# Router logits of two steps at once on column quarters, and three list products behind the transposes

## The chip, the cores and the metric

One core of one Trainium2 chip. The metric is device time in microseconds (us), the median of several executions. The engines are named as in the profile: PE is the matrix engine, PEld its weight loads, DVE the vector engine, ACT the scalar engine, POOL GpSimd, and SP the engine whose queue issues most of the transfers.

## What is computed

A retention layer (linear attention with a decay per head) over 4 batches of 768 tokens with 8 heads of 64, then a mixture of experts with a router in two levels. Cut to what matters:

```python
for t in range(S):                                   # B=4, H=8, S=768, D=64
    state = gamma * state + einsum('bhd,bhe->bhde', k[:, :, t], v[:, :, t])
    y[:, :, t] = scale * einsum('bhd,bhde->bhe', q[:, :, t], state)
x = y.transpose(0, 2, 1, 3).reshape(3072, 512)
g_logits = x @ w_group                               # 4 groups
g_idx = argmax(g_logits)
for g in range(4):
    e_logits = x[g_idx == g] @ w_expert[g]           # 4 experts in a group
    e_idx = argmax(e_logits)
    for e in range(4):                               # one expert for each token
        out[tok] = g_w * e_w * (relu(x[tok] @ w1[g, e]) @ w2[g, e])
```

The change is in the part that makes the 20 router logits of a token (4 of the groups, 16 of the experts).

## The kernel before, in words

The program has two stages. The first, `attention` (about 100 us), walks 12 steps; a step i holds two blocks of 128 tokens. The second runs the 16 experts with weights that stream from memory. A few instructions of the second (splitting the weights of the first expert) are laid between those of the first. The order on every engine is the order in which the code issues; no scheduler moves anything. So the line of a call in the loop of `attention` sets where it stands in each engine's queue.

A step i of `attention` issues on PE, in this order:

- `score_mm` of step i+1, first block (L240, PSUM banks sh0 and sh1), then `state_out` of step i (L291, queries by the state before), then `score_mm` of step i+1, second block (banks sh2 and sh3). DVE masks the scores out of the four banks into `pf` (`score_mask`, L252, four instructions a step); `pf` has three buffers, so the mask of the second block waits for the first half of step i's value product;
- `value_out` (L304, masked scores by values), then `state_mm` (L266, the new state), and ACT copies the state (L276). Steps 5 and 11 end a sequence, make no new state and need no keys; step 6 starts one and has no `state_out`. `state_mm` reads the keys from `kk`; for steps 9 and 10 (`KEYED`) these come by a transfer (L217), issued when the `state_mm` ahead of it is done; for the others PE transposes them (`keys_mm`, L225);
- `logits_mm` of step i-1 (L324): four products, one for each quarter of the 512 features, each with a stationary `wr` of 128x32 (20 columns used) and a moving `xt` of 128x256. Product j writes the 32 PSUM partitions 32j to 32j+31, so the four stand in four column quarters of the PE array, and each holds a part of the sum. ACT copies the 128x256 result to `ls` (L329). DVE makes `xt` in `out_x` (L316, two instructions a step);
- `keys_mm` of step i+1, then `trans_mm` of step i-1 (L350): `xt` transposed to token order, which ACT copies and SP writes to memory (`xd`);
- `select_mm` of step i-1 (L337): two products, stationary `ls` (128x128), moving a 0/1 matrix of 128x20, which add the four parts and turn the logits to one token a partition, in PSUM bank `log`. In steps 4, 8, 9 and 10 they are put off (`select_late`) into the step behind, among `score_mm`, `state_out` and `state_mm`.

Routing works on batches of two steps (`route`, a generator of small DVE instructions that `route_steps` advances). In an odd step, behind the masks, DVE makes the marks `oh` (L391 to L408) out of bank `log`; then `out_x`; behind the transposes PE counts ranks (L444, L446) into `log`, DVE reads them (L452 to L461), and in the even step weights follow (L421 to L434). `spread` (L527, L515 on DVE, L534 on POOL) and `tally` (L555, four bfloat16 products into `log`, and L562 on DVE, which adds them to `lists`) enter a batch into the experts' lists: `spread` at the end of steps 4, 6 and 8 and at the start of step 10, `tally` in steps 5, 7, 9 ahead of `state_out`, and in step 10.

All matrices of this stage but those of ranks and lists are float32. The trace shows a float32 product as two records, with a load each.

## Time and profile before

| what | us |
|---|---|
| median of 3 runs (394.51 to 395.0) | 394.56 |
| the profiled execution, its own time | 392.61 |
| its span, first to last instruction | 390.9 |

The span starts with the first instruction on any engine. The page lists busy time by engine, the chain of work that ended last (followed back from the end, at each step to what released it), and groups of instructions. The timeline lists instructions in order of time. Each view counts from the start of the span. The profiled execution is 1.95 us below the median of the runs.

### The profile page before, as it was taken

Reading aid. Unit: us, or ns where it says so; the run is one execution under the profiler, and the core shown is the slowest. Engines: PE = TensorE matmul, PEld = TensorE weight load, DVE = VectorE, ACT = ScalarE, POOL = GpSimd, SP = SyncE. Lnnn points to the kernel's source line nnn. Section 1 sums busy time; section 2 is a strip of 40 time slices with the busy share of each in tenths; the row PEclk is TensorE's granted clock in tenths of the full one; section 3 lists DMA queues with packets and bytes.
Section 4 is the critical chain, followed back from the end, with each engine's and each line's share of the span. In section 5 each row is a group of like instructions: output and inputs, shape, how many; then the busy total and the mean of one; then the engine's idle time right before and its main releaser. Section 6 shows DMA issues by size and latency. Waiting matters only on the chain.

```text
span 390.9 us, 14282 instructions
## 1 busy us (share of the span) xinstructions
PE 381.9 (98%) x5945; PEld 322.9 (83%) x5977; DVE 288.5 (74%) x480; ACT 224.3 (57%) x342; POOL 160.2 (41%) x172
## 2 busy tenths in 40 slices
PE   8999999999999999999999999999999999999993
PEld 4888989888869888888888879797887978879792
DVE  3675876868879979795868686776878769788630
ACT  2234534544654766666657667676766767667620
POOL 5533669578766325131425324241531403322112
PEclk9999999999999999999999999999999999999997
DMA  7999999989647998787879797988879798797011
GB/s 254 342 369 325 315 381 321 341 292 305 221 177 259 338 359 269 249 278 257 268 249 274 268 331 251 300 294 305 293 262 352 273 314 300 268 349 263 6 49 50
DMA packets 38042, 107.24 MB, mean 274 GB/s; under 512 B 11415, under 2 KB 11543, under 8 KB 30548
## 3 DMA queue, kind: packets, MB, share of 16 engines
q1 hardware_dynamic: 28752, 92.52, 68.5%
q0 software_dynamic: 8928, 12.63, 9.2%
q8 instruction: 54, 0.88, 0.9%
q10 hardware_dynamic: 292, 1.08, 0.8%
q14 instruction: 16, 0.13, 0.1%
HBM read 94.18 MB, written 13.20 MB: 275 GB/s over the span
## 4 chain that ended last, share of the span: by engine, by line
PE 83%; issue 9%; POOL 3%; DMA 3%; DVE 0%; POOLq 0%; ACT 0%; SPq 0%; DVEq 0%; ACTq 0%
PE hps L918 19%; PE yps L1011 16%; PE hps L898 9%; PE yps L1016 6%; PE op L304 5%; PE sh L240 4%; PE yps L1004 3%; PE tpx L839 3%; PE sh L350 3%; PE stp L266 3%; PE op L291 2%; POOL out L1098 2%; DMA kk<-kt 2%; PE sh L324 1%; PE yps L955 1%
## 5 line engine op out<-in xcount | busy, mean ns | idle before, releaser
L786 DVE TENSOR_TENSOR wl<-wf,wh 128x1024 bf16<-128x1024 f32 x120 | 145.3, 1222 | 38.5 <-ACT wh L784 38.2
L784 ACT ACTIVATE wh<-wf 128x1024 f16<-128x1024 f32 (+1 forms) x136 | 133.6, 1002 | 1.0 <-DMA wf<-w2p 1.0
L918 PE MATMUL hps<-xbh,wh 128*128 128x0 bf16 x544 | 93.3, 241 | 0.0
L918 PE MATMUL hps<-xbh,wl 128*128 128x0 bf16 x544 | 93.3, 241 | 0.0
L1098 POOL DMA_INDIRECT out<-yo,mt x18 | 22.2, 1235 | 102.9 <-ACT yo L1078 100.1
L918 PEld LDWEIGHTS <-wh 128*128 128x128 f16 x616 | 56.5, 98 | 0.1
L925 ACT ACTIVATE hh<-hps 128x256 bf16<-128x256 f32 (+16 forms) x68 | 34.2, 503 | 35.6 <-PE hps L918 35.3
L918 PEld LDWEIGHTS <-wl 128*128 128x128 bf16 x544 | 53.2, 98 | 0.2
L898 PE MATMUL hps<-xbl,wh 128*128 128x256 f16 (+14 forms) x472 | 50.2, 249 | 0.0
L1016 PEld LDWEIGHTS <-wh 128*128 128x128 f16 x448 | 28.6, 97 | 24.9
L252 DVE TENSOR_TENSOR pf<-sh,tri 128x512 f32<-128x512 f32 x48 | 30.6, 685 | 21.8 <-PE sh L240 7.8
L1011 PE MATMUL yps<-wh,hl 128*128 128x512 f16 x112 | 42.5, 380 | 0.0
L1011 PE MATMUL yps<-wl,hh 128*128 128x512 bf16 x112 | 42.4, 379 | 0.0
L1011 PE MATMUL yps<-wh,hh 128*128 128x512 f16 x112 | 42.4, 378 | 0.0
L821 POOL DMA_INDIRECT xg<-xd,mt x22 | 36.8, 1674 | 11.0 <-PE hps L898 2.7
L841 ACT ACTIVATE xbh<-tpx 128x512 bf16<-128x512 f32 (+14 forms) x32 | 16.7, 523 | 42.7 <-PE tpx L839 42.6
L898 PEld LDWEIGHTS <-wh 128*128 128x128 f16 x472 | 40.2, 98 | 0.5
L1016 PEld LDWEIGHTS <-wl 128*128 128x128 bf16 x448 | 28.6, 97 | 13.3
L928 DVE SCALAR_TENSOR_TENSOR hl<-hps,hh 128x216 f16<-128x216 f32 (+15 forms) x64 | 36.8, 576 | 2.7 <-ACT hh L925 2.6
L1098 POOL DMA_INDIRECT out<-yo,gx x8 | 9.5, 1194 | 55.6 <-ACT yo L1078 41.4
L1016 PE MATMUL yps<-hh,wh 128*128 128x0 bf16 x448 | 31.8, 192 | 0.0
L1016 PE MATMUL yps<-hh,wl 128*128 128x0 bf16 x448 | 31.7, 192 | 0.0
(210 smaller groups left out, 632.6 us busy)
## 6 DMA issues: line engine op xcount, KB each, us to landing
wf<-w2p SPq DMA_DIRECT2D x29, 1024.0 KB, 6.3
wf<-w1p SPq DMA_DIRECT2D x28, 1024.0 KB, 6.9
lq<-qkv SPq DMA_DIRECT2D x24, 256.0 KB, 5.8
lk<-qkv SPq DMA_DIRECT2D x24, 256.0 KB, 5.3
lv<-qkv SPq DMA_DIRECT2D x24, 256.0 KB, 5.8
xd<-xr SPq DMA_DIRECT2D x22, 256.0 KB, 4.9
wf<-w1p SPq DMA_DIRECT2D x16, 256.0 KB, 5.9
wf<-w2p SPq DMA_DIRECT2D x8, 256.0 KB, 5.9
```

The source lines that it names most:

```text
L252: nc.vector.tensor_tensor(o, sc, tri, ALU.mult)
L304: nc.tensor.matmul(s["o"][par][64 * half:64 * half + 64, u, pp], s["vs"][:, u, hs], s["pf", u][:, par, p, :], start=(c == 0 and u == 0 and ...
L784: nc.scalar.activation(u["wh"][i][:, cs], u["wf"][i][:, cs], AF.Copy)
L786: (eng or nc.vector).tensor_tensor(u["wl"][i][:, cs], u["wf"][i][:, cs], u["wh"][i][:, cs], ALU.subtract)
L821: nc.gpsimd.indirect_dma_start(out=xg[0:r, i, :], out_offset=None, in_=self.xd[0:n, :], in_offset=bass.IndirectOffsetOnAxis(ap=mt[0:r, i, ...
L898: nc.tensor.matmul(hv[:, a, 0:w], l, xl[:, k, 0:w], start=(k == 0 and a == 0), stop=False, skip_group_check=True)
L918: nc.tensor.matmul(o, l[:, k, fs], m, start=(n == 0 and not arms), stop=(n == len(terms) - 1), skip_group_check=True,)
L925: nc.scalar.activation(hh[:, f, 0:W], hv[:, :, 0:W], AF.Relu)
L928: nc.vector.scalar_tensor_tensor(*rest)
L1011: nc.tensor.matmul(big, h[:, k, 0:P], w[k], start=(n == 0), stop=(n == 23))
L1016: nc.tensor.matmul(o, w[k][:, d * P:d * P + P], m, start=(n == 0 and d == 0), stop=(n == 23), skip_group_check=True,)
L1098: s = nc.gpsimd.indirect_dma_start(out=self.out, out_offset=bass.IndirectOffsetOnAxis(ap=mt[0:r, i, 0:1].bitcast(U32), axis=0), in_=yo[0:r ...
```

## The change

- `logits_mm` and `select_mm` go, and with them the 0/1 matrix of the constants and `select_late`.
- `pair_logits(i)` makes the logits of steps i and i+1 together: 16 products, each with a stationary `wr` of 128x32 and one token block of `xt` as 128 moving columns. Column quarter j holds block j of the four, and the four feature quarters g are added up in PSUM. It is issued in even steps for the two steps before, behind the scores and ahead of `value_out`, into bank sh0; for steps 10 and 11 behind the loop.
- `pair_select` takes the place of four `select_mm` products: two, stationary `ls` (half the tokens of a block, 128x64), moving 80 columns of the identity matrix. It stands behind `state_copy` of the even step.
- `tally` of steps 5, 7 and 9 moves from ahead of `state_out` to behind `trans_mm`.

```diff
-                if i % 2 and not last:
-                    self.select_late()
-                if i in (5, 7, 9):
-                    self.tally()
                 if i > 2:
                     self.state_out(i, 0)
-                if last:
-                    self.select_late()
                 if i > 1:
                     self.state_out(i, 1)
-                if i < NS2 - 2:
-                    self.select_late()
                 if i % 2 == 0:
                     self.route_steps(99, True)
                 if i > 1:
                     scores(i + 1, 1)
+                if i % 2 == 0:
+                    self.pair_logits(i - 2)
...
             self.state_copy(i)
-            if i == 10:
-                self.select_late()
+            if i and i % 2 == 0:
+                self.pair_select()
             beside(i, 4)
-            if i:
-                self.logits_mm(i - 1, 1 if last or i % NC == NC - 2 or i + 1 in KEYED else 2)
             self.out_x(i)
...
             if i:
-                late = i + 1 in KEYED or i % NC == NC - 2
-                self.trans_mm(i - 1, late=late)
...
+                self.trans_mm(i - 1)
+                del self.st[i - 1]
+            if i in (5, 7, 9):
+                self.tally()
...
-            self.logits_mm(last)
+            self.pair_logits(last - 1)
             self.xtrans(ua, "big", (0,))
-            self.select_mm(last)
-            self.trans_mm(last, self.yp, late=True)
+            self.pair_select()
+            self.trans_mm(last, self.yp)
```

The new functions:

```diff
+    def pair_logits(self, i):
+        nc = self.nc
+        if i == NS2 - 2:
+            lt = self.pp.tile([P, 512], F32, name="lgt", tag="sta", bufs=1)[:, 0:P]
+        else:
+            lt = self.sh[0][:, 0:P]
+        for g in range(4):
+            for j in range(4):
+                nc.tensor.matmul(
+                    lt[32 * j:32 * j + 32, :], self.wr[:, g, :], self.xts[i + j // 2][:, g, j % 2],
+                    start=(g == 0), stop=(g == 3), skip_group_check=True,
+                )
+        self.ls = self.wp.tile([P, P], F32, name="ls", bufs=1)
+        nc.scalar.activation(self.ls, lt, AF.Copy)
+
+    def pair_select(self):
+        pick = self.ident.rearrange("p (j c) -> p j c", j=4)[:, :, 0:20]
+        for a in (0, 64):
+            lg = self.log[a:a + 64, LG:LG + 80].rearrange("p (j c) -> p j c", j=4)
+            self.nc.tensor.matmul(lg, self.ls[:, a:a + 64], pick, start=True, stop=True, skip_group_check=True)
```

Three places in the engines' queues (in the changed file the same code stands some lines earlier: L240, L266, L304, L555, L562 are L239, L265, L303, L548, L555 there).

PE in an even step, from the last score product to the key transposes; before (step 6):

```order
L240 MATMUL sh_118<-lq,lk 64x64
L240 MATMUL sh_119<-lq,lk 64x64
L304 MATMUL op<-pf,vs 64x128 x16
L266 MATMUL stp<-vs,kk 64x64 x16
L324 MATMUL sh_118<-xt,wr 32x256 x4
L225 MATMUL sh_116<-ident,lk 128x128 x4
```

and with the change:

```order
L239 MATMUL sh_118<-lq,lk 64x64
L239 MATMUL sh_119<-lq,lk 64x64
L326 MATMUL sh_116<-xt,wr 32x128 x16
L303 MATMUL op<-pf,vs 64x128 x16
L265 MATMUL stp<-vs,kk 64x64 x16
L338 MATMUL log<-ident,ls 64x80 x2
L224 MATMUL sh_116<-ident,lk 128x128 x4
```

The four products of 256 columns behind the state are now 16 of 128 columns ahead of the value product, in bank sh0 (`sh_116`), and two select products stand where the four stood. In an odd step neither stands any more.

DVE in step 7, where the list sum stands; before:

```order
L252 TENSOR_TENSOR pf<-sh_116,tri 128x512
L252 TENSOR_TENSOR pf<-sh_117,tri 128x512
L562 TENSOR_TENSOR lists<-lists,log 128x160
L252 TENSOR_TENSOR pf<-sh_118,tri 128x512
L252 TENSOR_TENSOR pf<-sh_119,tri 128x512
```

and with the change:

```order
L401 TENSOR_TENSOR oh<-log,go 128x64
L315 TENSOR_TENSOR xt<-op,gx 128x512 x2
L555 TENSOR_TENSOR lists<-lists,log 128x160
L445 TENSOR_TENSOR log<-log,nb 128x64
L448 TENSOR_TENSOR nb<-log,nb 128x16
```

The sum stood between the masks of the two score blocks; now it stands behind `oh` and `xt` and directly ahead of the reading of the ranks.

PE at the end of step 10; before:

```order
L350 MATMUL sh_118<-ident,xt 128x128 x4
L350 MATMUL sh_119<-ident,xt 128x128 x4
L291 MATMUL op<-lq,V 64x128 x8
L337 MATMUL log<-rest,ls 128x20 x2
L291 MATMUL op<-lq,V 64x128 x8
L304 MATMUL op<-pf,vs 64x128 x16
```

and with the change:

```order
L345 MATMUL sh_118<-ident,xt 128x128 x4
L345 MATMUL sh_119<-ident,xt 128x128 x4
L290 MATMUL op<-lq,V 64x128 x16
L303 MATMUL op<-pf,vs 64x128 x16
L845 TENSOR_LOAD ecols
```

The select products that split the state products of step 11 are gone.

## Rows read from the trace of the kernel before

**Rows 1.** Page, busy time by engine: us (share of the span) and instructions.

```profile
PE 381.9 (98%) x5945; PEld 322.9 (83%) x5977; DVE 288.5 (74%) x480; ACT 224.3 (57%) x342; POOL 160.2 (41%) x172
```

**Rows 2.** Chain that ended last, in order of time, step 7: start, us, what.

```profile
65.96 1.91 PE op L304 x32
67.87 0.93 PE stp L266 x32
68.81 0.57 PE sh L324 x8
69.37 1.02 PE sh L225 x8
70.40 0.87 PE sh L350 x8
71.27 0.36 PE log L337 x4
71.63 0.04 PE log L444
...
71.76 0.81 PE sh L240 x24
72.57 0.89 PE op L291 x32
73.46 0.65 PE sh L240 x24
```

**Rows 3.** The same chain, step 5's list products; the select products put off to step 11.

```profile
48.54 0.28 PE log L555 x4
48.82 1.03 PE op L291 x32
...
94.63 0.79 PE op L291 x16
95.42 0.55 PE log L337 x4
95.98 0.60 PE op L291 x16
```

**Rows 4.** Timeline, step 4's logits products on PE and their loads: start, us, engine, line, what.

```profile
45.49 0.16 PEld L324 LDWEIGHTS sh<-xt,wr 128*32 128x32 f32 x8
45.49 0.64 PE L324 MATMUL sh<-xt,wr 128*32 128x256 f32 x8
```

**Rows 5.** Line L324, its loads: duration of one, ns, least, median and most.

```profile
L324 PEld LDWEIGHTS sh<-xt,wr x88: 106/108/110, 19.4 to 98.4; 128*32 128x32 f32 x88
```

**Rows 6.** Timeline, steps 9 and 10: start, us, engine, line, what.

```profile
80.65 0.31 DVE L562 TENSOR_TENSOR lists<-lists,log 128x160 f32<-128x160 f32 x1
...
81.85 1.97 PE L304 MATMUL op<-pf,vs 128*64 128x128 f32 x32
...
83.06 1.29 DVE L252 TENSOR_TENSOR pf<-sh,tri 128x512 f32<-128x512 f32 x2 [2.10 <-PE op L304]
...
86.33 1.28 DVE L316 TENSOR_TENSOR xt<-op,gx 128x512 f32<-128x512 f32 x2
...
87.52 0.22 DVE L452 TENSOR_TENSOR log<-log,nb 128x64 f32<-128x64 f32 x1
...
89.73 0.79 DVE L527 TENSOR_TENSOR yT<-rest,tile 128x128 bf16<-128x128 f32 x1
...
91.05 2.47 DVE L252 TENSOR_TENSOR pf<-sh,tri 128x512 f32<-128x512 f32 x4
```

**Rows 7.** The chain again, step 5: value product and rank product.

```profile
50.51 1.06 PE op L304 x16
...
55.78 0.04 PE log L444
```

**Rows 8.** The chain again, the transfer of the keys of step 9.

```profile
77.59 6.23 DMA kk<-kt
...
83.87 1.33 PE stp L266 x32
```

## The prediction, on record before the changed kernel ran

> **What bounds the kernel now.** I read the page first: PE is busy 98% of the span [rows 1], so in general a microsecond less on PE is a microsecond less in all. Then the chain of work that ended last, over the first 100 us. It runs through PE nearly without a break, so in this stage the chain's rows are prices: each is the time by which a group of products moves the end. Step 7 shows a whole step [rows 2]: value product 1.91, state 0.93, logits 0.57, key transposes 1.02, `xt` transposes 0.87, select 0.36, ranks 0.13 (from 71.63 to 71.76), then scores 0.81, state products 0.89, scores 0.65. The step's last row ends where the next value product starts. The third view is the timeline of DVE in the odd steps [rows 6]: there DVE does masks, marks, `xt` and the reading of the ranks one behind the other, and a PE that gets shorter meets a DVE that doesn't.

> A second price stands in the same rows. Transposes behind other transposes take 0.87; of the same count and shape behind the column quarters of the logits they take 1.02 [rows 2]. Scores behind transposes take 0.81, behind state products 0.65. So a change between whole array, halves and quarters costs about 0.15.

> **PE work removed.** Twelve logits groups at 0.57 [rows 2]: 6.84. Twelve select groups: six behind transposes at 0.36 [rows 2], the six others near the 0.55 of the one in step 11 [rows 3]: 5.4. That one also cuts the state products in two: 0.79 and 0.60 [rows 3] in place of 0.89 [rows 2], so 0.5 goes with it. The list products of steps 5, 7 and 9 stand between scores and state products, and behind them the state products take 1.03 [rows 3] against 0.89 [rows 2]; behind transposes no change of shape is left: 3 x 0.14, 0.4. Sum 13.1.

> **PE work added.** `pair_logits`, six times 16 float32 products with 128 moving columns, in four column quarters. The nearest rows are the state products: 16 products, 128 columns, four parts of the array at once, 0.89 [rows 2]. Halving the length of L324 gives the upper end: 16 products of 128 columns are as many columns as two groups of four with 256, 2 x 0.57 = 1.14 [rows 2]. The lower end is 0.85, the 0.89 without its own edges. I take 0.89 and 0.15 for a change of shape, 1.04: the row has the same count of products and of parts. Six of them: 6.24. `pair_select`: two products of 80 columns in two halves, behind the state products, which have the same halves and take 0.93 for 16 of 64 columns [rows 2], 0.058 each. 2 x 0.058 x 80/64 = 0.15, between 0.1 and the 0.36 of today's select. Five of them 0.75; the sixth stands between transposes behind the loop and pays two changes of shape, 0.45. Added in all 7.4, so PE sheds 13.1 - 7.4 = **5.7 us**.

> [...]

> **Waits that it adds.** *Rank products.* They write bank `log`, and so do the list products; the list sum on DVE reads it. In the built program the list products now wait for `oh`, and the first rank product waits for the list sum. That sum stands behind `xt` on DVE. Step 9 gives DVE's times from the start of the value product at 81.85 [rows 6]: second mask at 1.2 (it needs the `pf` buffer that the first half of the value product frees), `xt` from 4.5 to 5.75, so the list sum (0.31 [rows 6]) ends at 6.06, and the ranks start there. Steps 5 and 7 have the same DVE work. PE would be there sooner:
> - step 7: 1.91 + 0.93 + 1.02 + 0.87 + 0.28 for the list products [rows 2, 3] = 5.01. Wait 1.05; before, the ranks came at 5.67 with none [rows 2].
> - step 5 makes no state: 4.08, wait 1.98. Before, its ranks came at 55.78 - 50.51 = 5.27 [rows 7], of which 1.91 + 0.57 + 1.02 + 0.87 + 0.36 = 4.73 is work, so 0.54 is not new: 1.44.
> - step 9 has no key transposes: 1.91 + 0.93 + 1.02 + 0.28 = 4.14, wait 1.92, of which about 0.35 was there (ranks 4.78 behind the value product, work 4.43): 1.57. The transfer of its keys hides in this. It is issued when the state of step 8 is done and takes 6.23 [rows 8]; PE gets to the next state some 0.9 us before it lands, and waits there in place of waiting at the ranks.

> Together 4.06. Queued behind the waiting rank product on PE are the scores, the state products and the pair's logits, and through them the next value product.

> *Logits in step 10.* `pair_logits` writes sh0, so it waits for the first mask of scores that were made just before. In step 10 DVE first finishes the route and the `spread` of steps 6 and 7: from reading the ranks at 87.52 to the masks at 91.05 it takes 3.53 [rows 6], and 0.65 more for the first mask. With 0.13 for the ranks themselves, `pair_logits` can start 4.31 behind their start. PE is there after 0.13 + 0.81 + 0.89 + 0.65 = 2.48 [rows 2]. Wait 1.83, all new: today the value product stands there and needs only masks of the step before. In steps 2, 4 and 8 the mask is ready (DVE has no `spread` in front of it); in step 6, without state products, it is 0.15 late.

> *Behind.* In step 11 the ranks lose the 0.57 of logits that stands ahead of them, and their marks come no sooner; I take 0.5, between 0 and 0.57. For the logits behind the loop, which wait for the last `xt`, 0.1.

> Sum of the waits: 4.06 + 1.83 + 0.15 + 0.6 = **6.6 us**. Costed at nothing: the smaller copy on ACT (ACT has slack, 57% [rows 1]); the later first pair of logits, since `route` starts at the end of the even step as before; the loads of q, k and v, which move with the steps. The experts' stage is bound by PE and shifts as a whole.

> **Sum.** -5.7 + 6.6 = +0.9. The profiled execution would go from 392.6 to 393.5. That execution lies 1.95 below the median of the runs; on the median the forecast is 394.56 + 0.9 = **395.5 us**. What a measurement can tell from no change is 0.2%, 0.8 us, here.

> **Rivals.**
> - *The waits just eat the work.* The same mechanism with DVE a little quicker: the `yT` in step 10 took 0.79 [rows 6] beside POOL, and in another alignment it may be shorter; the wait at step 11 may be 0. Then +0.9 - 0.5 - 0.5 = -0.1, 394.5, no measurable change. For it: my sum is a small difference of two large ones. Chance 0.32.
> - *Faster: DVE's work ahead of the first mask in step 10 is short enough.* It decides at 2.5 us from ranks to finished mask: below that the 1.83 is gone, and the kernel is at 395.5 - 1.8 = 393.7. Against it stand the rows: 3.53 for that stretch, and DVE's order there is unchanged. For it: part of the stretch waits for POOL. Chance 0.17.
> - *PE alone bounds.* The list products find their marks ready and the ranks find the sum ready: -5.7 and the small waits, about 389.4. The order on DVE, where the sum stands behind `xt`, speaks against it. Chance 0.04.
> - *The loads are laid bare in `pair_logits`*, as if rounds on the same rows could not overlap: 0.86 more in each of six groups [rows 5], 395.5 + 5.2 = 400.7. Rows 4 speak against it. Chance 0.04. [...]

> That the change doesn't do what it says I leave out: the order shows the products gone and the new ones in place.

> **How the numbers follow.** Forecast 0.43, the others as given. Slower by over 0.2%: 0.43 + 0.04 = 0.47; within: 0.32; faster: 0.17 + 0.04 = 0.21. The slower case alone runs from 395.4 to 397.3: upper end with 1.14 for the logits (+0.6), 0.36 for the select (+1.0) and waits as computed. The range of 8 in 10 goes on down through no change to the faster case, 393.0, and leaves out the two rivals with 0.04 and a tail: **393.0 to 397.3**.

> **What would show it.** Right: L326 groups of about 1.0 on the chain, selects of 0.15 to 0.2; in steps 5, 7 and 9 the rank products (L437) start 6.0 to 6.2 behind the value product, just behind the list sum; in step 10 PE idle of 1.5 to 2.2 ahead of L326 with a DVE mask as what ended it; the even-to-odd halves of a pair shorter by about 1.4 and the odd-to-even longer. Wrong: no idle time at these places, or an L326 group of 1.5 or more, or a last attention step that ends more than 1.5 us from where it ends now while the list above holds.

## The result, and the profile after

The changed kernel takes 399.03 us (median of 10 runs, 396.43 to 401.45) against 394.63 for the kernel before in the same session (10 runs, 393.07 to 395.81): ratio 1.0108, 95% interval 1.0075 to 1.0142. It is slower by 4.4 us. The forecast was 395.5 with a range up to 397.3: the sign is right, the size is not. The profiled execution took 398.88, close to the median.

The page, busy time by engine, against [rows 1]:

```profile
span 397.1 us, 14370 instructions
...
PE 377.4 (95%) x5974; PEld 322.3 (81%) x6049; DVE 288.6 (73%) x480; ACT 221.5 (56%) x336; POOL 159.3 (40%) x172
```

PE did get shorter by 4.5 us, 381.9 to 377.4. But the span grew, so PE is idle for 10.7 us more than before (397.1 - 377.4 = 19.7, against 390.9 - 381.9 = 9.0). The question is what it is idle for. The chain that ended last, steps 2, 3 and 6 and 7 (start, us, what), against [rows 2]:

```profile
26.13 0.65 issue
26.78 0.66 PE sh L239 x15
27.44 1.01 PE sh L326 x32
28.45 1.90 PE op L303 x32
30.35 0.93 PE stp L265 x32
31.28 0.14 PE log L338 x4
31.42 1.02 PE sh L224 x8
32.44 0.11 PE sh L345
32.55 1.35 issue
33.90 0.98 PE sh L345 x7
...
60.04 1.08 PE sh L326 x32
61.12 1.90 PE op L303 x32
63.02 0.93 PE stp L265 x32
63.95 0.14 PE log L338 x4
64.09 1.03 PE sh L224 x8
```

The prices of the two new groups came out: L326 1.01 to 1.08 (forecast 1.04), L338 0.14 (forecast 0.15). Beside them stand rows named "issue", which [rows 2] don't have: PE stands still in the middle of a group of like products, and no engine and no transfer of data ended it. The waits of PE by line, from 8 us to the end of the attention stage (us in total, times, longest):

```profile
PE log L437 <- DVE lists L555: 2.3, 3, 1.0
PE sh L326 <- DVE pf L251: 2.1, 2, 1.9
PE sh L345 <- issue: 1.3, 1, 1.3
PE op L290 <- issue: 0.9, 2, 0.6
PE sh L239 <- issue: 0.6, 1, 0.6
PE stp L265 <- issue: 0.4, 1, 0.4
PE op L303 <- issue: 0.4, 1, 0.4
PE sh L224 <- DVE m L394: 0.3, 1, 0.3
```

The first two rows are the waits that the prediction named. The others it didn't have.

**Where the unexplained stalls stand.** I counted all records on TensorE's own queue in the trace, products and weight loads and the few others, in order of start. In all seventeen profiles of this study the stalls that no engine explains stand at record 193, 449, 705 and so on: 256 records apart, though not at each of these places. Everywhere else in the attention stage a wait of over 0.15 us has a releaser that fits, but for one of 0.28 us in E10. The page's queue list shows a queue of 55 instruction packets, 0.90 MB, 16.4 KB each.

```profile
q8 instruction: 55, 0.90, 0.9%
```

A page is here a block of 256 records, and a border is the first record of a page, at 193, 449 and so on. The packets keep step with the borders: in the changed kernel's profile there are seventeen borders from 9.96 to 101.68 us, and between each two neighbours exactly one of these packets starts. So I take each packet for the next page. The table is worked out from the packet times and the records of the changed kernel, in us; "stall there" is the stall at the next border.

```
border at  packet starts after  packet takes  packet's end to next border  stall there  page lasted
  9.96          3.49               0.97                1.43                  0.89         5.90
 15.86          2.36               0.92                1.78                  0            5.06
 20.92          3.55               1.02                1.29                  0.91         5.86
 26.78          4.92               0.98                1.22                  1.62         7.12
 33.90          1.80               0.96                1.79                  0            4.55
 48.39          3.22               0.94                1.25                  0.68         5.41
 83.17          2.82               0.93                1.47                  0.67         5.22
```

A page's packet starts 1 to 5 us after the border before it, takes about 1 us (up to 1.6), and the page's first record never runs less than 1.1 us behind the packet's end, 1.2 to 1.5 in the stalled ones. My reading, which no view names: where PE is through with a page earlier than some 1.2 us behind the packet's end, it waits for the next one. In the attention stage a page lasts about 5.5 us, and the start of its packet, the packet and these 1.2 us come to 4.0 to 7.1 by the rows above, so the sum is just hidden, or just not. I call these page stalls. The other profiles agree: at 269 borders of this stage in the seventeen of them, no record runs less than 1.1 us behind its packet's end, and all 81 stalls of over 0.3 us end 1.2 to 1.65 us behind it.

**The ledger.** For each profile I split the time from the first state product of the attention stage (L291, L290 after) to the first transposes of the experts' stage (L839, L832): page stalls (a gap of over 0.15 us between two starts at a record 193 of 256, less 0.05), other gaps (more than 0.36 us between two starts, less a usual 0.2), and the rest, which is products at work. "Before again" is a second profile of the kernel before (E16 below), since the first is of an execution 2 us below the median.

```
kernel                  records  page stalls  other gaps   rest   sum
before, first profile     3873      0.57         0.32      86.02   86.91
before again (E16)        3873      2.12         0.50      86.09   88.70
changed                   4020      5.71         4.77      81.12   91.60
```

From before again to changed: products -5.0, waits for engines +4.3, page stalls +3.6. That is +2.9.

Not every page stall moves the end. Three of them (0.68, 0.58 and 0.67, in steps 5, 7 and 9) stand between the start of the value product and the rank products, and one of 0.24 stands in step 11. There the chain that ended last runs through DVE, as in step 5:

```profile
52.13 1.06 PE op L303 x16
...
53.29 1.29 DVE pf L251 x2
...
56.49 1.28 DVE xt L315 x2
57.76 0.24 DVE lists L555
...
58.05 0.20 PE log L437
```

By this chain PE would have waited for DVE in place of these stalls, which are 2.0 us together. Counted by what moved the end, the split is products -5.0, waits for engines +6.2, page stalls +1.6. For the same reason the column of page stalls is an upper bound of what they cost in those of the kernels that have such waits.

Another 1.3 us was lost behind, in the experts' stage (289.4 to 290.7 from its first transposes to the end). Of it 0.6 lie ahead of PE's last product, of which one piece can be seen, the last list product, which now waits for POOL; 0.7 lie behind that product, where the profiles differ between 6.5 and 7.5 us, also those with the list work of before (E16 6.5, E10 7.5), so this part can't be laid to the change:

```profile
119.35 0.44 PE L548 MATMUL tally<-gx 128*128 128x160 bf16 x4 [0.42 <-POOL gx L527]
```

### The profile page after: what moved, and what is told of

Read it like the earlier page. It is cut to its first block, busy times and chain, and to the rows that moved or that the text cites. A ratio compares the mean times of both kernels' runs of the same rounds, so it can differ in the third digit from the quotient of the medians.

```text
span 397.1 us, 14370 instructions
## 1 busy us (share of the span) xinstructions
PE 377.4 (95%) x5974; PEld 322.3 (81%) x6049; DVE 288.6 (73%) x480; ACT 221.5 (56%) x336; POOL 159.3 (40%) x172
## 3 DMA queue, kind: packets, MB, share of 16 engines
q10 hardware_dynamic: 292, 1.08, 0.8%
## 4 chain that ended last, share of the span: by engine, by line
PE 74%; issue 11%; DVE 5%; POOL 4%; DMA 4%; ACT 0%; POOLq 0%; SPq 0%; DVEq 0%; ACTq 0%
PE hps L911 18%; PE yps L1004 14%; PE hps L891 9%; PE yps L1009 8%; PE op L303 4%; PE sh L239 4%; PE yps L997 3%; PE tpx L832 3%; PE op L290 2%; POOL out L1091 2%; PE stp L265 2%; PE sh L345 2%; DVE pf L251 2%; DMA xg<-xd,mt 1%; PE sh L326 1%
## 5 line engine op out<-in xcount | busy, mean ns | idle before, releaser
L196 POOL TENSOR_TENSOR vs<-lv,cst 128x512 f32<-128x512 f32 x24 | 24.6, 1042 | 16.3 <-DMA lv<-qkv 9.9
```

What stands on the lines that cost most here:

```text
L196: self.nc.gpsimd.tensor_tensor(o, v, g, ALU.mult)
```

## The experiments

The theories by their letters: A, the dense stretch of short instructions ahead of the value product outruns their supply; B, only the new waits for VectorE cost time and the unexplained stalls are chance. After E1 to E4, when neither held: S, PE waits for its next page wherever a page is used up too fast; W, products and waits for engines are all; F, a page takes its time whatever else is moved.

Times are medians beside runs of the kernel before in the same session. Ratios to those, with their 95% intervals, are worked out from the single runs, so they differ a little from a ratio of medians. Sessions differ: before stood at 394.76 us for E1 to E4, at 397.26 for E5 and E7 to E9, at 394.62 for E10 to E13 (the same chip as the session ahead of it) and 394.10 for E14 to E16. In the session at 397.26 the experts' stage takes 291.9 to 293.9 us in every profile, elsewhere 289.4 to 290.7, so across sessions only ratios and ledgers compare. Their ledgers (the rest of E2 and E11 also holds 6.8 us at half the granted clock, that of E9, E13 and E14 3.4 us, so it is not products alone; see the last section):

```
kernel                              records  page stalls  other gaps   rest   ratio to before
E1  logits behind value product       4026      7.63         2.58      81.49   1.0066
E2  list products forward             4019      4.94         5.01      85.32   1.0105
E3  before, list products back        3873      4.79         2.35      85.71   1.0070
E4  both moves undone                 4021      6.23         1.13      82.84   1.0053
E5  E4, wide pairs                    3831      4.20         2.14      84.01   1.0018
E7  E4, fewer loads                   4021      4.97         1.55      83.25   1.0012
E8  before, fewer loads               3873      1.68         0.97      85.94   0.9970
E9  changed, fewer loads              4021      5.11         2.73      82.53   1.0089
E10 before, cheap selects             4065      4.98         1.72      85.99   1.0074
E11 E4 shifted                        4022      6.15         1.41      85.58   1.0129
E12 before shifted                    3873      0.85         1.44      85.70   1.0134
E13 changed shifted                   4021      6.42         6.59      82.83   1.0252
E14 changed, wide pairs               3830      3.25         6.58      84.24   1.0138
E15 before, more records              4017      3.62         0.00      86.73   1.0089
E16 before again                      3873      2.12         0.50      86.09   1.0008
```

### E1 to E4: each move undone

E1, the router products behind the value product:

```diff
-                if i % 2 == 0:
-                    self.pair_logits(i - 2)
...
             self.value_out(i, 1)
+            if i and i % 2 == 0:
+                self.pair_logits(i - 2)
```

> The changed kernel with the sixteen router products of two steps taken from ahead of the value product to behind it, same products, same steps. Theory A (TensorE's instructions: in even steps 64 score, 64 state-out, 64 score and 64 router instructions follow one another in 3.4 us, faster than a 16 KB instruction packet follows a page of 256 instructions; the issue stalls of 0.5 to 1.6 us, some 5 us in all against 0.5 before, are the larger half of the loss): the mask waits ahead of the router products (2.2 us in step 10, 0.4 in step 6) go, and most of the issue stalls of even steps too, though value and router products are now neighbours; 392 to 394 us. Theory B (only the new waits for VectorE, the gaps without a releaser are chance): the mask waits go, the issue stalls stay at about 5 us, 396 to 397 us.

Measured 397.64 (12 runs), ratio 1.0066 (1.0040 to 1.0092). The mask waits went, as both theories said; the page stalls did not, they grew. One stands inside the value product (timeline on PE):

```profile
77.14 0.66 PE L303 MATMUL op<-pf,vs 128*64 128x128 f32 x8
79.33 1.53 PE L303 MATMUL op<-pf,vs 128*64 128x128 f32 x24 [1.53 <-issue]
```

So the dense stretch ahead of the value product is not the cause by itself, as theory A had it: A's number, 392 to 394, fell. B's 396 to 397 was nearer, but B took the stalls for chance.

E2, the list products of steps 5, 7 and 9 forward again:

```diff
+                if i in (5, 7, 9):
+                    self.tally()
                 if i > 2:
                     self.state_out(i, 0)
...
-            if i in (5, 7, 9):
-                self.tally()
```

> The changed kernel with the list products of steps 5, 7 and 9 back ahead of the state-out product, everything else as changed. Both theories: the three waits of the rank products (1.2, 0.6 and 1.1 us, 3.0 in all) go, 0.4 us of shape changes come back: 396 to 397 us. Theory A: the issue stalls stay (about 5 us), and the runs still spread over some 4 us. A third theory C, that the list products' place is the whole loss through the gather that it holds up: 394.5 us.

Measured 399.25 (6 runs), ratio 1.0105 (1.0061 to 1.0150): no gain, a miss for all three theories. The wait changed its name. PE's waits by line:

```profile
PE sh L326 <- DVE pf L251: 2.9, 2, 2.4
PE sh L326 <- issue: 2.2, 1, 2.2
PE log L548 <- POOL yT L527: 1.6, 2, 0.8
PE log L437 <- DVE oh L401: 0.9, 2, 0.6
```

PE, with less to do, reaches the list products before POOL has their matrix, and the router products later still before the mask. This profile, of an execution of 401.96, also shows what the granted clock does behind PE's two longest idle times, told at the end.

E3, the kernel before with the list products behind the transposes, the reverse of E2's edit:

> The kernel before with nothing but the list products of steps 5, 7 and 9 put behind the x transposes. If the wait of the rank products for VectorE's list sum costs what it measures: +1.5 to +2.6 us, 396.1 to 397.2 us (a gap of 0.6 to 1.2 us ahead of the rank products in each of three steps, 0.4 us of shape changes saved). If PE makes it up later: 394.4 us. Theory A: no new issue stalls of over 0.4 us, since the router products stay split.

Measured 397.88 (8 runs), ratio 1.0070 (1.0045 to 1.0095), +2.8 us, a little above the 1.5 to 2.6 expected of the wait alone: the wait is not made up later. The three gaps ahead of the rank products are 0.66, 0.64 and 1.20. But A's "no new issue stalls" fell: the profile has 4.79 us of page stalls against 2.12, and two of them, at 15.04 and 26.69 us, stand in a part of the program that is the same as before. So part of a profile's page stalls is chance.

E4, E1 and E2 together:

> The changed kernel with both moves taken back: router products of two steps behind the value product and the list products ahead of the state-out product, so that the saving in products is left. Theory A: 389 to 391 us, faster than the kernel before by about 4 us (5.7 us less work in products, 0.4 of it given back, little waiting). Theory B: 393 to 394 us, since the issue stalls stay.

Measured 397.12 (12 runs), ratio 1.0053 (1.0025 to 1.0082). Both theories missed. Other gaps are down to 1.13 us and the products are 3.2 us shorter than in E16, yet it is slower: page stalls of 6.23. One of them shows how such a stall can be misread:

```profile
69.60 1.10 PE L265 MATMUL stp<-vs,kk 128*64 128x64 f32 x32
72.58 1.09 PE L224 MATMUL sh<-ident,lk 128*128 128x128 f32 x8 [1.88 <-DVE oh L401]
```

The view puts it down to DVE's `oh`, which ended just then. But the product is record 193 of its page, and the page's packet had ended 1.26 us earlier. Key transposes have no business with `oh`.

### E5, E7 to E9: fewer records, fewer loads

E5 is E4 with the router products of two steps as eight of 256 columns, 192 records fewer over all:

```diff
-        for g in range(4):
-            for j in range(4):
-                    lt[32 * j:32 * j + 32, :], self.wr[:, g, :], self.xts[i + j // 2][:, g, j % 2],
-                    start=(g == 0), stop=(g == 3), skip_group_check=True,
+        for g in range(2):
+            for j in range(4):
+                    lt[32 * j:32 * j + 32, :], self.wr[:, j % 2 * 2 + g, :],
+                    self.xts[i + j // 2][:, j % 2 * 2 + g].rearrange("p u t -> p (u t)"),
+                    start=(g == 0), stop=(g == 1), skip_group_check=True,
```

> E4 with the router products of two steps as eight of 256 columns by feature quarters instead of sixteen of 128, and two selections that sum two quarters each: about the same columns, but 32 fewer TensorE records for each pair of steps, 192 in all, three quarters of a 256-record page. In the runs so far all issue stalls of over 0.35 us stand at the same place of a page of 256 records. Theory S (TensorE waits for its next page, whose 16 KB packet stands among 2.5 MB of loads and stores per step): fewer records, fewer or shorter stalls, 393 to 395 us. Theory W (the time follows the products' work and the waits for other engines): as E4, 397 us.

Ratio 1.0018 (0.9983 to 1.0053; 398.39, 12 runs, in the session with 397.26), between the two theories' numbers. Against E4's 1.0053, on another chip, the direction is S's: page stalls 6.23 to 4.20 though its products take 1.2 us more. The two intervals overlap.

E7 (E4), E8 (before) and E9 (changed) leave out half of the weight pieces that steps 2 to 9 load:

```diff
-                        for k in range(2):
-                            self.wload_part(ua, 2 * i - 4 + k)
+                        self.wload_part(ua, 2 * i - 4)
```

> E4 with one of the two 256 KB weight pieces that each of steps 2 to 9 loads left out (the odd pieces of expert 0's weights aren't read: its even pieces are used twice, so its outputs differ); the same instructions on TensorE, VectorE, ScalarE and GpSimd. 2 MB less in the attention stage, about 10%. Theory S: page packets start sooner after the crossing (3.3 to 4.3 us at the stalls of E4), the stalls (6.5 us) fall below 2 us, and the saving in products shows: 390 to 392 us. Theory F (a page takes its time whatever else is moved, or the stalls are chance): 396 to 397 us.

> The kernel before with the same weight pieces left out (expert 0's outputs differ). Both theories: TensorE is bound by its own work in the attention stage and had 0.6 us of page stalls there: 393.5 to 394.5 us. If it comes out at 392 or less, data waits in the kernel before were more than its trace tells.

> The changed kernel with the same weight pieces left out (expert 0's outputs differ). Theory S: the page stalls (6 us) go, the waits for the list sums and masks stay: 394 to 395.5 us. Theory F: 398 to 399 us.

Ratios 1.0012 (0.9979 to 1.0045), 0.9970 (0.9944 to 0.9997) and 1.0089 (1.0050 to 1.0128). Each stands 0.2 to 0.4% under its full-load sister, also before's; but E4 and the changed kernel ran in other sessions, and their intervals overlap with those of E7 and E9. S had promised that the stalls go; they fell from 6.23 to 4.97, and 5.71 to 5.11. So 2 MB less to load, of some 31 MB moved (before, 8 to 103 us: 325 GB/s), is not what makes packets early; the loads are at most a part of the packet's delay.

### E10: no new wait, only other products

The kernel before, each step's logits at their old places, but in the block layout; its list products unmoved:

```diff
-        for j in range(4):
-                lt[32 * j:32 * j + 32, :], self.wr[:, j, :], s["xt"][:, j].rearrange("p u t -> p (u t)"),
+        for g in range(2):
+            for j in range(4):
+                f = j % 2 * 2 + g
+                    lt[32 * j:32 * j + 32, :], self.wr[:, f, :], s["xt"][:, f, j // 2],
...
-        for u in range(2):
-            nc.tensor.matmul(lg, s["ls"][:, u * P:u * P + P], self.rest[:, C_SEL:C_SEL + 20], start=True, stop=True)
+        for a in (0, 64):
+            nc.tensor.matmul(
+                lg, s["ls"][:, a:a + 64], self.rest[:, C_SEL:C_SEL + 40], start=True, stop=True, skip_group_check=True
+            )
```

> The kernel before with each step's logits kept at their places, but as eight products of 128 columns by token block and feature half, and two selections of 64 tokens by 40 columns: no product waits for another step, a mask or a list sum that it did not wait for before; 96 fewer columns' worth of weight load in the selections, 16 more records per step in the logits (192 in all). Theory W (the new waits of the change are what cost it): the cheap selections show in full, about 4 us, 390 to 391 us at a before of 394.7. Theory S (pages of 256 TensorE records arrive late as soon as a page is used up faster): most is given back in page stalls, 393 to 395 us.

Measured 398.26 (12 runs), ratio 1.0074 (1.0038 to 1.0110), worse than either theory's number. The cheap selections did not show: the rest is 85.99 us, as in E16. That makes it the cleaner comparison: the same products' time, no new wait on DVE, 192 records more, and 2.9 us slower. Page stalls are 4.98 against 2.12, nine of them over 0.15 us, and the largest other gap is a gather ahead of the experts' stage. PE's waits by line:

```profile
PE tpx L843 <- DMA xg<-xd,mt: 1.4, 1, 1.4
PE op L304 <- issue: 1.0, 2, 0.8
...
```

### E11 to E13: the program moved by half a page

```diff
-WARM = 9
+WARM = 4
...
+        for i in range(69):
+            nc.tensor.matmul(warm[0:32, 0:8], one[:, 0:32], one[:, 0:8], start=True, stop=True)
```

> E4 with its TensorE records moved by half a page: 5 of the 9 warming products ahead of the first load replaced by 69 tiny ones, 128 records more in the time in which TensorE waits for its first load anyway. Theory S: every stall that no engine explains moves by 128 records with the pages (to place 65 of 256, from 193), its sum changes (6.2 us in E4, between 2 and 9 us here) and the time with it, by 1 to 4 us either way. Theory W: nothing changes by more than 1 us.

> The kernel before with the same shift by 128 records. Theory S: the place of the page borders among the loads was favourable (0.6 us of stalls in its profile, and its shortest pages of 4.2 us met packets that came early); moved by half a page it has 2 to 5 us: 395.5 to 399 us. Theory W: 394.7 us, as before.

> The changed kernel with the same shift by 128 records. Theory S: its 5.7 us of page stalls change, 395 to 402 us, at other places (65 of 256); the waits for list sums and masks stay. Theory W: 399 us, as the changed kernel.

Ratios 1.0129 (1.0087 to 1.0170), 1.0134 (1.0093 to 1.0175) and 1.0252 (1.0195 to 1.0308). These times can't be used as meant, since fewer long warming products changed the start as well. E12's timeline on PE has slower first products, the group of 32 scores in 1.56 us against 0.90 elsewhere, and its first state product 4.3 us later than E16's (18.98 against 14.70):

```profile
2.63 2.00 PE L169 MATMUL warm<-const-bfloat16-1.0 128*32 128x8 bf16 x69
5.91 1.56 PE L242 MATMUL sh<-lq,lk 64*64 64x128 f32 x32 [1.27 <-DMA lk<-qkv]
```

Only the ledger behind that is of use. Page stalls stayed at records 193 of 256 (my "place 65" was a slip: borders are counted from the first instruction, so the program moves and the borders don't). Before still had few, 0.85; E4 and the changed kernel still had about 6. So it matters little which products stand at a border; S as an accident of alignment falls.

### E14 to E16: records alone

E14 is the changed kernel with E5's wide products. E15 is the kernel before with three tiny products more per step:

```diff
+        for j in range(3):
+            nc.tensor.matmul(
+                lt[32 * j:32 * j + 32, 0:16], self.wr[:, j, :], s["xt"][:, j, 0, 0:16],
+                start=True, stop=True, skip_group_check=True,
+            )
```

> The changed kernel with nothing but its router products as eight of 256 columns by feature quarters, as in E5: in the same place, behind the same mask waits, 1.2 us more work in products and selections over all, 192 TensorE records fewer. Theory S (records per page): page stalls fall from 5.7 us to 2 to 4, 397 to 398.5 us at a before of 394.7. Theory W (work and waits for engines alone): 399.5 to 400.5 us.

> The kernel before with three tiny router products of 16 columns more per step, overwritten by the real ones behind them: 12 TensorE records per step, 144 in all, as many as the change adds. Their own work: about 0.1 us per step by the tiny selections of the changed kernel (8 records in 0.14), 1.2 to 2 us in all. Theory S: besides, page stalls rise by 1.5 to 4 us: 397.5 to 400 us. Theory W: their work alone, 396 to 396.7 us.

> The kernel before, unchanged, for a second profile (the first is of an execution 2 us faster than the median). Both theories: the time of before within 0.3 us. Theory S: page stalls of 1 to 3 us, below all eight profiles of programs with the change's records (4.9 to 7.6); if it shows 5 us or more, the stalls don't go with the records.

E14: 399.89 (6 runs), ratio 1.0138 (1.0106 to 1.0170), W's number. Its page stalls fell as S said, 5.71 to 3.25, but the rest rose by 3.1 us, not 1.2, and the other gaps by 1.8. The other gaps grew in steps 5, 7 and 9, where no page stall stands ahead of the list and rank products any more and PE waits for DVE instead. The rest holds a stretch at half the granted clock, behind the mask wait of step 10, in which the value product takes 3.47 us in place of 1.97 (timeline, then the windows view with the fields as in the last section):

```profile
96.39 3.47 PE L303 MATMUL op<-pf,vs 128*64 128x128 f32 x32
```

```profile
96.65:100.06 3.41, 3.41 (x40) 3.41 (x38) 1.80 (x3) 0.26 (x1) 2.10 (x3) 0.50 0.71 264
```

That is 1.5 of the 3.1. Over E14's six runs the mean granted clock is 0.992, against 0.996 to 0.997 in the runs of before. So the time at W's number is no support for W.

E15: 397.55 (6 runs), ratio 1.0089 (1.0058 to 1.0121), +3.5 us, S's number. Three tiny products take 0.15 to 0.16 us on the chain, at most 1.9 us in all; in the ledger the rest rose by 0.6. Page stalls 3.62 against 2.12, in an execution of 396.35, below its median. The granted clock is no rival here: its mean over the runs is 0.996. All that PE waits for in this stage:

```profile
PE op L291 <- issue: 0.5, 1, 0.5
PE log L342 <- issue: 0.4, 1, 0.4
PE op L304 <- issue: 0.4, 1, 0.4
PE sh L324 <- issue: 0.4, 1, 0.4
PE sh L240 <- issue: 0.2, 1, 0.2
```

E16: 394.53 (12 runs), ratio 1.0008 (0.9989 to 1.0028), with 2.12 us of page stalls:

```profile
PE sh L240 <- issue: 0.9, 1, 0.9
PE op L291 <- issue: 0.6, 1, 0.6
PE sh L350 <- ACT ls L329: 0.2, 1, 0.2
```

Over all profiles: the four of the kernel before and its shifted or lighter forms (E8, E12, E16) have 0.57 to 2.12 us of page stalls; the eight with the paired narrow products have 4.94 to 7.63; E10 and E15, before's products with more records, 4.98 and 3.62; E5 and E14, with fewer records and shorter products, 4.20 and 3.25. E3, at 4.79 with before's records, is the one that doesn't fit. So page stalls go with the rate of records, with a good deal of chance on top. The single pages say the same: over all seventeen profiles the pages that end in a stall would have lasted 5.05 us without it (median), the others last 5.54; and their next packet started 3.4 us behind the border, in the others 2.2.

No version beat the kernel before. The nearest with all the work, E5, can't be told from it.

## Why the prediction was right or wrong

- **Products removed and added: right in kind, 0.7 too large.** -5.7 forecast, -5.0 measured in the ledger against E16. L326 and L338 came out at their forecast; where the 0.7 is lost was not followed up.
- **Loads laid bare: it did not happen.** L326's loads run beside its products, as the L324 rows [rows 4] had them: in step 6 the 32 loads stand from 60.04 on in 0.81 us, beside products that run from 60.04 for 1.08. With the rival's 0.86 on top, eight loads of 0.108 [rows 5], a group would have taken some 1.9 us; 1.01 to 1.08 stands in the chain.
- **Rank products behind the list sum: right in place and kind, a little too large.** They start 5.92, 5.94 and 5.91 us behind the value product in steps 5, 7 and 9 (forecast 6.0 to 6.2). The wait is 2.3 us in all against a forecast of 4.06, since page stalls of 0.68, 0.58 and 0.67 (steps 5, 7 and 9) stand ahead of them on PE and use up 1.8 of it. Wait and stalls together are 4.1; but the 4.06 left out 0.9 us that the prediction took to be in before already, of which E16's other gaps show 0.5.
- **Logits of step 10 behind the mask: right.** 1.93 against 1.83, ended by DVE's mask; step 6 0.21 against 0.15:

```profile
95.49 1.08 PE L326 MATMUL sh<-xt,wr 128*32 128x128 f32 x32 [1.93 <-DVE pf L251]
```

- **The sum of the waits, 6.6, came out at 4.3**, and at 6.2 with the page stalls that stand in the place of such waits. With products at -5.0 that is +1.2 where the forecast had +0.9, so the terms that the sum had were nearly right. What failed is the step "Costed at nothing" and the sum that rests on it: PE's time was taken as products plus waits for other engines, and PE's own instructions were in no list. They cost 3.6 us more than before, of which 1.6 moved the end. With it failed "the experts' stage ... shifts as a whole" (1.3, of which 0.7 may be chance) and 0.7 of the saving in products. Less the 0.4 by which the waits stayed under their forecast, that is 3.2 of the miss of 3.5. Saved products were paid back twice: PE came earlier to DVE's results, and it came earlier to the ends of its pages, with 144 records more on its queue.
- **"That execution lies 1.95 below the median of the runs".** I carried this over as an offset. E16 shows that most of it was page stalls (2.12 against 0.57): the profile I argued from was the lucky one, and had hidden the cost that the change would raise. Its chain had one such row, 0.35 us of "issue" at 14.65, and I did not ask what it was:

```profile
14.65 0.35 issue
```

- **"The experts' stage ... shifts as a whole".** It grew by about 1.3 us. One wait of 0.42 in it is shown above, 0.7 stand behind PE's last product; the small remainder is not followed up.
- The last sign listed as wrong, an attention stage that ends over 1.5 us from where it ended while the list above it holds, is what happened.

**Left open.** What makes a packet start 1.08 us after a border in one case and 4.92 in another, in the same profile. Loads explain little (E7 to E9), position little (E11 to E13). And S is shown as a tendency over seventeen profiles, not as a price for each record: E3 doesn't follow it, and E14's time is set by its waits and its clock.

## What to carry to other kernels

In the kernel before PE was busy for 98% of the span with short instructions, and in the changed one its instruction stream set part of the time, with page stalls of 5.71 us against 2.12. In such a kernel count the records that a change adds, and how long 256 of them last (5.05 us in the pages that ended in a stall, 5.54 in the others), beside the time of its products. A stall named "issue", or one put down to an engine that the instruction has nothing to do with, is worth counting records for. Cutting PE's work bought nothing here while the next two limits, the mask and list work on DVE and the pages, stood where they were: products -5.0 us, waits for engines +4.3, page stalls +3.6.

## What was not expected of the hardware

The granted clock fell behind some of the longest idle times of PE. In E2 a stall of 2.22 us ended at 77.44, and the value product behind it took 2.79 us instead of 1.97, at a granted clock of 0.50 (windows: PE, loads, DVE, ACT, POOL busy, granted clock, DMA share, GB/s):

```profile
77.44 1.50 PE L326 MATMUL sh<-xt,wr 128*32 128x128 f32 x22 [2.22 <-issue]
78.87 2.79 PE L303 MATMUL op<-pf,vs 128*64 128x128 f32 x32
```

```profile
77.40:79.00 1.60, 1.56 (x24) 1.17 (x25) 0.00 (x0) 0.01 (x1) 1.06 (x5) 0.50 1.05 384
```

So such a wait can cost more than itself, here 0.8 us in the value product alone. The same happened behind the mask wait in step 10 of E2, E13 and E14, behind a page stall of 2.11 us in E11 (6.83 us at half), and in E9 some 2 us behind one of 1.91; but not in the changed kernel's own profile, whose wait there was as long as E14's (1.93; granted clock 1.00 from 95 to 100 us). The mean granted clock over the runs is 0.995 in the changed kernel and 0.996 to 0.997 in the four sessions' runs of before. By an estimate from these means the clock costs the changed kernel some 0.7 us more than before in an average run; its profiled execution has no stretch at half in the attention stage, so the ledger holds none of this. Whether it is part of why the changed kernel's runs spread over 5.0 us and before's over 2.7 was not tested.
